# A joint ring for the q and k projections, 1 KB weight rows in two slots, and a smaller preference for attention in the list scheduler

## The chip, the core and the metric

The kernel runs on one core of a Trainium2 chip. The metric is the device time of one execution in microseconds. The core has five engines with a queue of instructions each: TensorE (PE, matmuls), VectorE (DVE), ScalarE (ACT), GpSimd (POOL) and SyncE (SP). Every engine works through its queue in order; between engines there are semaphores. DMAs are issued from the queues of SP and POOL and carried out by 16 DMA engines that both share.

## The reference, cut to what matters

```python
x = A_x                                  # 1 x 2048 x 576, bf16
xn = _layernorm(x)
s = _A_ref(xn, A_wqkv, A_wo)             # attention: 32 heads of 18, each query sees the 256 keys up to itself
g = _silu(_B_ref(xn, w_gate, w_up, w_down))
return x + s * g

# _A_ref
qkv = (x @ wqkv).reshape(B, S, 3, H, Dh)         # D = 576, so q, k and v have 576 columns each
scores = einsum(q, k) * Dh ** -0.5, masked to 0 <= i - j < 256
o = softmax(scores) @ v
return o @ wo
# _B_ref, F = 4608
h = sigmoid(x @ w_gate) * (x @ w_up)
return h @ w_down
```

## The kernel before, in words

**Tiling.** The 2048 tokens are cut into four chunks of `NT` = 512. For each chunk the builder makes the operations of one pipeline: layer norm and transposes into `xnT` (`build_ln`), the v projection (`build_v`), the q/k projection (`build_qk`, five column groups `gi` of 128), attention for eight head groups `hg` of four heads (`build_attn`), the output projection (`build_wo`) and the FFN (`build_ffn`). All contractions over 576 are done as nine pairs of matmuls with 64 rows each; the two of a pair run side by side in the upper and lower half of the array (`pair`, line 88, which is why nearly all of TensorE's work has that line).

**q and k.** `build_qk` projects 128 columns of q and of k at once into one PSUM unit, and a VectorE copy (line 517) puts them into `qd[:, slot, 0 or 1, :]`, a ring of two slots. Heads are 18 columns wide and the attention wants each at a multiple of 32 partitions, so every head is spread by DMA: one from the q half into `qT` (a ring of four slots, one per head group in flight), one from the k half into `kT`. All of these are issued from POOL's queue through the helper `dma` (line 232). `kT` holds, for every head group, three units of 256 keys; two hold the current chunk and one the second half of the chunk before, and `unit_slot` and `sub_pos` say which. The projection of group `gi` needs the slot of `qd` that the spreads of `gi - 2` have to have read. `build_attn` then makes `kx`, two copies of all 768 keys with every second head set to zero (line 595, two VectorE instructions per head group, ring of two), computes five batches of scores, exponentials on ScalarE (line 626), masks on VectorE, and the product with v (`pv`).

**FFN.** F = 4608 is 36 tiles of 128 (`ft`). `weights(wg)` loads the columns of `WG` = 2 tiles of gate (to partitions 0 to 63) and of up (to 64 to 127) into one of `NWS` = 4 slots of `wgs` with two DMAs from SP's queue; a row of such a load is 2 x 128 x 2 bytes = 512 B. A slot is released when its last tile has been multiplied. `gate_up` is one half of a tile's gate/up work, `tail` the tanh and the product that give `hT`. `down` is the second projection, `build_final` the gate, the residual and the store. In chunk 0 the first three tiles are worked in two halves of the tokens before the attention can begin. All weights are read again in every chunk, except `wd_sb`, which stays.

**Order.** Nothing is ordered by hand. `schedule` is a list scheduler that runs at build time with estimated durations: at each step it takes, for the engine that can start earliest, the operation with the least `start + prio * PRIO_NS`; attention has priority 1, gate/up and down steps 3. It estimates 600 ns for a DMA's issue, lands it 2.5 us later, and not before the bytes of all earlier DMAs have passed at 205 bytes per ns. The order it finds is then fixed for every engine: a step whose operand is later than planned stops everything behind it on its engine.

```python
DMA_ISSUE_NS = {"SP": 600.0, "POOL": 600.0, "ACT": 650.0}
DMA_LAT_NS = 2500.0
DMA_BYTES_PER_NS = 205.0
...
k = (st + o.prio * self.PRIO_NS, o.cidx)
```

The functions that the diff touches, and what calls them:

Of the kernel before, what the change touches and what calls it, by code (L numbers as in the profile page):

```python
# [20 lines left out]
BPC = NT // P  # L21
FG = 4
NFG = NFT // FG
WG = 2
NWS = 4
EPS = 1e-5
SM_SCALE = float(DH) ** -0.5

# [2 lines left out]
NVS = 12  # L31
VH = DH + 1
VSZ = (H // 2) * VH
NOT = 1
NQS = 4
NKX = 2
NEX = 8
# [25 lines left out]
def mm_ns(n):  # L63
    return max(24.7, n / 2.4 + 2.7)
# [136 lines left out]


class Builder:
    PRIO_NS = 80.0

    def __init__(self, nc, x_ap, wqkv_ap, wo_ap, wg_ap, wu_ap, wd_ap, out_ap, verbose=False):
        self.nc = nc
# [28 lines left out]
    def alloc_memory(self):  # L236
        nc = self.nc
        bf16, f32 = dt.bfloat16, dt.float32
        cur = [(nc.sbuf_base + 63) // 64 * 64]
        top = nc.sbuf_top  # L240

        def size(shape, dtp):
            n = 1
            for s_ in shape[1:]:
                n *= s_
            return n * mybir.dt.size(dtp)

        def seq(name, shape, dtp=bf16, align=32):
            off = (cur[0] + align - 1) // align * align
            cur[0] = off + size(shape, dtp)  # L250
            assert cur[0] <= top, f"out of SBUF at {name}: {cur[0]} > {top}"
            return nc.alloc_sbuf_tensor_at(name, list(shape), dtp, offset=off), off

        self.xnT, _ = seq("xnT", [P, 2, KS, NT])
        self.wd_sb, _ = seq("wd_sb", [P, NFT, D])
        self.hT, _ = seq("hT", [P, NFT, NT])
        self.wgs, _ = seq("wgs", [P, NWS, 9, WG * P])
        self.tring, _ = seq("tring", [P, 2, NT])
        self.v_aug, _ = seq("v_aug", [P, NVS * VSZ + VH])
        self.qT, _ = seq("qT", [P, NQS, NT])  # L260
        self.kT, _ = seq("kT", [P, NHG, 12 * SW])
        self.kx, _ = seq("kx", [P, NKX, 12, 2, SW])
        self.expr, zex = seq("expr", [P, NEX, 2, NT])
        self.x0 = nc.alloc_sbuf_tensor_at("x0", [P, BPC, D], bf16, offset=zex)
        assert size([P, BPC, D], bf16) <= size([P, NEX, 2, NT], bf16)
        self.o_tok, _ = seq("o_tok", [P, BPC, XW])
        self.oT, _ = seq("oT", [P, NOT, KS, P])
        self.s_attn, _ = seq("s_attn", [P, BPC, D])
        self.wqk, _ = seq("wqk", [P, KS, XW])
        self.wv_sb, _ = seq("wv_sb", [P, KS, D // 2])  # L270
        self.wo_sb, _ = seq("wo_sb", [P, KS, D // 2])
        self.qd, _ = seq("qd", [P, NQD, 2, NT])
        self.xr, _ = seq("xr", [P, NXR, D])
        self.xnr, _ = seq("xnr", [P, NXN, XW])
        self.xf, _ = seq("xf", [P, NFIN, D])
        self.thf, _ = seq("thf", [P, NFIN, D])
        self.ident, _ = seq("ident", [P, SW])
        self.mask, _ = seq("mask", [P, P])
        self.small, _ = seq("small", [P, 3 + 16 * NST], f32)
        sm = self.small  # L280
        self.neghalf, self.half = sm[:, 0:1], sm[:, 1:3]
        self.bnst = sm[:, 3:3 + 12 * NST].rearrange("p (s i c) -> p s i c", i=2, c=6)
        self.mv = sm[:, 3 + 12 * NST:3 + 14 * NST].rearrange("p (s c) -> p s c", c=2)
        self.veps = sm[:, 3 + 14 * NST:3 + 15 * NST].rearrange("p (s c) -> p s c", c=1)
        self.rstd = sm[:, 3 + 15 * NST:3 + 16 * NST].rearrange("p (s c) -> p s c", c=1)
        self.pvs, _ = seq("pvs", [P, 1, 4 * BPC * (DH + 1)], f32)
        if self.verbose:
            print(f"SBUF used up to {cur[0]} of {top} ({top - cur[0]} free)")
        self.ps = nc.alloc_psum_tensor("ps", [P, 4096], f32)
        self.psb = self.ps.bitcast(bf16)  # L290
        self.pool_s = Pool("S", [0, 1])
        self.pool_f = Pool("F", [2, 3])

    def build_graph(self):
# [14 lines left out]
        self.op_xnT = [[] for _ in range(NC)]  # L309
        self.op_v = {}  # L310
        self.op_vis = {}
        self.op_kx = {}
        self.last_vis = None
        self.ffn_last = None
        self.op_pv = {}
# [85 lines left out]
    def build_attn_consts(self):  # L401
# [3 lines left out]
        o = op("POOL", 400, lambda e: e.memset(vv[:, :, DH:VH], 1.0), "init:vones", deps=d, prio=1)  # L405
        self.op_vones = o
        self.op_vzero = o = op("POOL", 100, lambda e: e.memset(self.v_aug[:, NVS * VSZ:NVS * VSZ + VH], 0.0), "init:vzero", deps=[o], prio=1)
        self.op_qz = o = op("POOL", 1600, lambda e: e.memset(self.qT[:, :, :], 0.0), "init:qz", deps=[o], prio=1)
        self.op_kz = o = op("POOL", 6200, lambda e: e.memset(self.kT[:, :, :], 0.0), "init:kz", deps=[o], prio=1)
        lo = slice(0, SW)  # L410
        o = op("POOL", 150, lambda e: e.memset(self.mask[lo, :], 1.0), "init:m0", deps=[o], prio=1)
        o = op("POOL", 200, lambda e: e.affine_select(self.mask[lo, 0:SW], self.mask[lo, 0:SW], pattern=[[-1, SW]],
# [83 lines left out]
    def build_qk(self, c, gi):  # L496
# [24 lines left out]
        for u in range(H):  # L521
            lo, hi = max(DH * u, gi * P), min(DH * u + DH, (gi + 1) * P)
            if lo >= hi:
                continue
            hg, p0 = u // 4, 32 * (u % 4) + lo - DH * u
            for w in range(2):
                if w == 0:
                    if (c, hg) not in self.q_slot:
                        self.q_slot[(c, hg)] = self.r_q.produce()
                    qs, war = self.q_slot[(c, hg)]  # L530
                    war = [war, self.op_qz]
                    dst = self.qT[p0:p0 + hi - lo, qs, :]
                else:
                    war = [self.op_kx[(c - 1, hg)]] if c else [self.op_kz]
                    n1 = unit_slot(c, 1)
                    dst = self.kT[p0:p0 + hi - lo, hg, :].rearrange("p (u t) -> p u t", u=3)[:, 0:n1 + 1:n1, :]
                s0, sb = (lo - gi * P, w) if gi < 4 else (lo - gi * P + 64 * w, 0)
                src = self.qd[s0:s0 + hi - lo, sq, sb, :]
                if w:
                    src = src.rearrange("p (u t) -> p u t", u=2)  # L540
                o = self.dma(dst, src, (hi - lo) * NT * 2, f"dma:sp:{c}:{u}:{w}:{gi}", ("qk", par, gi),
                             deps=[ev, war], prio=1, eng="POOL")
                self.op_sp.setdefault((c, hg), []).append(o)
                self.sp_grp.setdefault((c, gi), []).append(o)
                self.r_qd.release(sq, o)
                self.hg_grps.setdefault((c, hg), set()).add(gi)

    def row_proj(self, eng, h, lhs, w):
        res = None
# [34 lines left out]
    def build_attn(self, c, hg):  # L584
# [4 lines left out]

        sx, dx = self.r_kx.produce()  # L590
        kxo = []
        for t in range(2):
            def f_kx(e, t=t):
                src = self.kT[:, hg, :].rearrange("p (s k) -> p s k", k=SW)
                return e.tensor_scalar(self.kx[:, sx, :, t, :], src, self.half[:, t:t + 1], None, ALU.mult)  # L595
            kxo.append(op("DVE", dve_ns(12 * SW, 4.0), f_kx, f"kx:{c}:{hg}:{t}", deps=[sp, dx, self.op_kz, self.op_half], prio=1))
        self.op_kx[(c, hg)] = kxo

        where = {}
        ready = []  # L600
# [1 line left out]
        for vi, (specs, groups) in enumerate(zip(bins, masks)):  # L602
# [3 lines left out]
            def f_sc(eng, specs=specs, h=h):  # L606
                res = None
                outs = self.halves(h, NT)
                for ks, q0, nq in specs:
                    kp = sub_pos(c, ks)  # L610
                    cols = slice(q0 * SW, (q0 + nq) * SW)
                    res = pair(eng, [b[:, cols] for b in outs],
                               lambda r, t: self.kx[r, sx, kp, :, :].rearrange("p t k -> p (t k)"),
                               lambda r, t: self.qT[r, qs, cols], True, True)
                return res
            sc = op("PE", sum(mm_ns(nq * SW) for _, _, nq in specs), f_sc, f"sc:{c}:{hg}:{vi}",
                    deps=[sp, kxo, self.r_ex.rel[self.r_ex.uses % NEX]], prio=1, acq=h, odeps=[self.last_vis])
# [36 lines left out]
        def f_pv(eng):  # L654
# [22 lines left out]
                    res = pair(eng, [b[:, o + VH:o + 3 * VH].rearrange("p (k d) -> p k d", k=2) for b in outs],  # L677
                               lambda r, i: self.expr[r, se, t, qb * P:(qb + 1) * P], two, True, True)
            return res
        pv = op("PE", 40 * 24.7, f_pv, f"pv:{c}:{hg}", deps=[[m for m, _ in ready], vdeps, self.op_vzero], prio=1, acq=hp)  # L680
        self.op_pv[(c, hg)] = pv
        for se in sorted({se for _, se in ready}):
            self.r_ex.release(se, pv)
# [67 lines left out]
    def build_ffn(self, c):  # L751
# [13 lines left out]

        def weights(wg):
            sw, dw = self.r_w.produce()
            pr = 1 + wg if c == 0 and wg < 4 else 3
            fc = slice(wg * WG * P, (wg + 1) * WG * P)
            ds = self.load_rows(self.wgs[:, sw, :, :], self.wg[:, fc], self.wu[:, fc], f"dma:w:{c}:{wg}", ("w", sw), pr, [dw])  # L770
            slots[wg] = sw
            wops[wg] = ds

        def load_wd(fg):
            self.op_wd.append(self.dma(
# [8 lines left out]
        def gate_up(ft, h, half, acq, part=None):  # L784
# [6 lines left out]
            def f(eng):  # L791
                res = None
                outs = [bank(h, w)[:, t0:t0 + n] for w in range(2)]
                for k in ks:
                    res = pair(eng, outs, lambda r, t: self.wgs[r, sw, SUB[t][k], fc], lambda r, t: x_in[r, k, t0:t0 + n],
                               k == 0, k == KS - 1)
                return res
            return pe(len(ks) * mm_ns(n), f, f"f1{half}:{c}:{ft}", [xin, wops[ft // WG]], acq,
                      3 if part is None else 1)

        def tail(ft, h, pg):
# [12 lines left out]
        if early:  # L814
            weights(0)
            weights(1)
            hs = [self.pool_f.hold() for _ in range(2)] + [self.pool_s.hold()]
            for part in range(2):
                for ft in range(early):
                    gate_up(ft, hs[ft], 0, None if part else hs[ft], part)  # L820
                    u = gate_up(ft, hs[ft], 1, None, part)
                    if part:
                        tail(ft, hs[ft], u)
                    if part and ft == 1:
                        self.r_w.release(slots[0], u)
        for ft in range(early, NFT):
            if ft % WG == 0 and ft // WG not in slots:
                weights(ft // WG)
# [266 lines left out]
```

## Time and profile before

| | |
|---|---|
| time, median of three | 591.35 us (590.41 to 591.4) |
| span of the profiled execution | 591.4 us |
| TensorE's granted clock, mean | 0.995 |
| gate/up matmuls (`ps<-xnT,wgs`) | 2646, 302.6 us of records |
| down matmuls (`ps<-wd_sb,hT`) | 2304, 153.4 us |
| spreading DMAs issued by POOL | 144 to `qT` (75.8 us), 144 to `kT` (80.7 us) |
| `kx` multiplies on VectorE, 768 columns | 64, 24.5 us |
| weight loads `wgs` | 144 of 288 KB |

A span of a matmul in the trace holds its whole way through the array, so that neighbours overlap; what a stretch of matmuls costs is read from the starts. A pair of 64 x 512 matmuls follows the one before it after 216 ns. In the page, L88 is any matmul, L232 any DMA issue; the names of the tiles tell them apart. `SPq` and `POOL` with DMA_DIRECT2D are issues, not transfers.

### The profile page before, as it was taken

The page shows a single profiled execution, that of the slowest core. Times are in us where ns is not written, and L with a number is a line of the kernel's source. Part 1 is how long each engine was busy: PE and PEld are TensorE (multiplying, and loading weights), DVE is VectorE, ACT ScalarE, POOL GpSimd, SP SyncE. Part 2 cuts the span into 40 slices and gives each one's busy share as a digit, 9 for nine tenths or more (in the row PEclk, how much of TensorE's full clock was granted, in tenths as well). Part 3 has the DMA queues.
Part 4 walks back from the last instruction along what each step waited for, and adds up shares of the span by engine and source line. Part 5 has one row for each costly group of instructions (what it writes and reads, how often), then busy time and mean ns, then how long its engine had stood idle before and what let it go on. Part 6 is the DMA issues. An engine that isn't in the chain of part 4 may idle for free.

```text
span 591.4 us, 21879 instructions
## 1 busy us (share of the span) xinstructions
PE 575.2 (97%) x9774; PEld 366.3 (62%) x9774; DVE 347.7 (59%) x832; ACT 279.8 (47%) x389; POOL 173.7 (29%) x318
## 2 busy tenths in 40 slices
PE   8889999999999999999999999999999999999996
PEld 7545555687785556456677765555557864444775
DVE  5447869964679878477776347887631233333122
ACT  3234857642378774267775247668420022332111
POOL 5495630007980300984200296450000000000000
PEclk9999999999999999999999999999999999999999
DMA  9999998731214553456301025465461116763010
GB/s 200 193 214 195 202 184 198 175 87 40 71 28 102 118 147 82 105 125 139 91 4 43 8 53 131 121 138 121 112 156 32 32 44 154 166 161 81 2 43 21
DMA packets 112046, 63.82 MB, mean 108 GB/s; under 512 B 12208, under 2 KB 109936, under 8 KB 111952
## 3 DMA queue, kind: packets, MB, share of 16 engines
q1 hardware_dynamic: 102736, 57.67, 43.2%
q0 software_dynamic: 9216, 4.75, 4.0%
q8 instruction: 77, 1.26, 1.0%
q14 instruction: 17, 0.14, 0.1%
HBM read 55.30 MB, written 2.36 MB: 97 GB/s over the span
## 4 chain that ended last, share of the span: by engine, by line
PE 89%; DMA 4%; POOL 3%; SPq 2%; DVE 1%; issue 1%; ACT 0%; DVEq 0%
PE ps L88 88%; DMA kT<-qd 2%; DMA wqk<-in_A_wqkv_dram 2%; SPq L232 2%; POOL qT L232 1%; POOL kT L232 1%; PE ps L480 1%; DVE qd L517 0%; DVE s_attn L890 0%; DVE thf L895 0%; DVE hT L806 0%; ACT tring L803 0%; DVE xf L900 0%; DVE xnr L451 0%; DVEq L1023 0%
## 5 line engine op out<-in xcount | busy, mean ns | idle before, releaser
L88 PE MATMUL ps<-xnT,wgs 64*128 64x512 bf16 (+1 forms) x2646 | 302.6, 372 | 2.7 <-DVE xnr L451 1.4
L88 PEld LDWEIGHTS ps<-xnT,wgs 64*128 64x128 bf16 x2646 | 128.8, 94 | 123.5 <-DVE xnr L451 1.5
L626 ACT ACTIVATE expr<-ps 128x1024 bf16<-128x1024 f32 (+2 forms) x160 | 152.4, 985 | 51.2 <-PE ps L88 50.9
L88 PE MATMUL ps<-wd_sb,hT 64*128 64x288 bf16 x2304 | 153.4, 283 | 1.3 <-issue 1.3
L806 DVE SCALAR_TENSOR_TENSOR hT<-tring,ps 128x512 bf16<-128x512 bf16 x144 | 98.8, 686 | 84.4 <-ACT tring L803 81.4
L803 ACT ACTIVATE tring<-ps 128x512 bf16<-128x512 f32 x144 | 86.2, 599 | 114.5 <-PE ps L88 111.9
L88 PEld LDWEIGHTS ps<-wd_sb,hT 64*128 64x128 bf16 x2304 | 111.4, 94 | 28.3 <-issue 1.6
L232 POOL DMA_DIRECT2D qT<-qd x144 | 75.8, 528 | 118.1 <-PE ps L88 74.9
L232 POOL DMA_DIRECT2D kT<-qd x144 | 80.7, 562 | 11.8 <-DVE qd L517 11.4
L639 DVE TENSOR_TENSOR expr<-expr,mask 128x256 bf16<-128x256 bf16 (+2 forms) x232 | 62.5, 292 | 30.3 <-ACT expr L626 29.1
L692 DVE TENSOR_REDUCE pvs<-ps 64x304 f32<-64x608 f32 x64 | 50.4, 788 | 10.7 <-PE ps L88 9.5
L88 PE MATMUL ps<-qT,kx 64*128 64x320 bf16 (+4 forms) x736 | 56.7, 252 | 0.0
L880 ACT ACTIVATE thf<-ps 128x576 bf16<-128x576 f32 (+1 forms) x20 | 11.1, 555 | 76.2 <-PE ps L88 75.9
L88 PEld LDWEIGHTS ps<-qT,kx 64*128 64x128 bf16 x736 | 30.8, 94 | 24.7 <-issue 2.5
L88 PE MATMUL ps<-xnT,wqk 64*128 64x512 bf16 (+1 forms) x360 | 39.4, 363 | 5.7 <-DMA kT<-qd 2.7
L88 PEld LDWEIGHTS ps<-v_aug,expr 64*128 64x128 bf16 x2432 | 35.2, 93 | 6.4 <-issue 0.8
L443 POOL TENSOR_TENSOR small<-small 128x1 f32<-128x1 f32 x16 | 9.2, 580 | 94.0 <-DVE small L441 93.9
L88 PE MATMUL ps<-v_aug,expr 64*128 64x19 bf16 (+1 forms) x2432 | 36.0, 170 | 0.2 <-issue 0.2
L88 PEld LDWEIGHTS ps<-xnT,wqk 64*128 64x128 bf16 x360 | 18.1, 95 | 23.7 <-issue 8.1
L883 DVE SCALAR_TENSOR_TENSOR thf<-thf,ps 128x576 bf16<-128x576 bf16 x12 | 9.0, 749 | 38.2 <-ACT thf L880 38.1
L517 DVE CAST qd<-ps 128x1024 bf16<-128x1024 f32 (+1 forms) x20 | 22.3, 1116 | 13.2 <-PE ps L88 13.1
L595 DVE TENSOR_SCALAR kx<-kT,small 128x768 bf16<-128x768 bf16 x64 | 24.5, 408 | 5.8 <-DMA kT<-qd 5.2
(52 smaller groups left out, 262.2 us busy)
## 6 DMA issues: line engine op xcount, KB each, us to landing
wgs<-in_B_w_gate_dram SPq DMA_DIRECT2D x72, 288.0 KB, 4.0
wgs<-in_B_w_up_dram SPq DMA_DIRECT2D x72, 288.0 KB, 4.9
wd_sb<-in_B_w_down_dram SPq DMA_DIRECT2D x9, 576.0 KB, 8.9
xf<-in_A_x_dram SPq DMA_DIRECT2D x16, 144.0 KB, 2.2
out_dram<-xf SPq DMA_DIRECT2D x16, 144.0 KB, 1.8
qT<-qd POOLq DMA_DIRECT2D x112, 18.0 KB, 2.6
kT<-qd POOLq DMA_DIRECT2D x112, 18.0 KB, 2.5
xr<-in_A_x_dram SPq DMA_DIRECT2D x6, 288.0 KB, 3.9
```

The source lines that it names most:

```text
L88: res = eng.matmul(outs[i], lhs(ROWS[t], i), rhs(ROWS[t], i), start=start, stop=stop, tile_position=(64 * t, 0))
L232: o = self.op(eng, DMA_ISSUE_NS[eng], lambda e: e.dma_start(dst, src), name, deps, prio, nbytes=nbytes)
L443: rs = op("POOL", 560, lambda e, ss=ss: e.tensor_tensor(self.rstd[:, ss, :], self.veps[:, ss, :], self.neghalf[:, :], ALU.pow), f"ln:rs:{s ...
L517: return eng.tensor_copy(dst, self.both(h, n))
L595: return e.tensor_scalar(self.kx[:, sx, :, t, :], src, self.half[:, t:t + 1], None, ALU.mult)
L626: return eng.activation(self.expr[:, se, :, lo * SW:NT], self.both(h, NT)[:, :, lo * SW:NT], ACTF.Exp, scale=SM_SCALE)
L639: return eng.tensor_tensor(e_, e_, m_, ALU.mult)
L692: return eng.tensor_reduce(out[ROWS[i]], src, mybir.AxisListType.X, ALU.add)
L803: th = op("ACT", act_ns(NT), lambda e: e.activation(self.tring[:, st, :], bank(h, 0), ACTF.Tanh, scale=0.5), f"th:{c}:{ft}", deps=[pg, dt_ ...
L806: mu = op("DVE", dve_ns(NT), lambda e: e.scalar_tensor_tensor(self.hT[:, ft, :], self.tring[:, st, :], 1.0, bank(h, 1), ALU.add, ALU.mult) ...
L880: return e.activation(v2(t)[:, a:b, :], y2()[:, a:b, :], ACTF.Tanh, scale=0.25)
L883: q1 = op("DVE", dve_ns(D), lambda e: e.scalar_tensor_tensor(v2(t), v2(t), 1.0, y2(), ALU.add, ALU.mult), f"fq1:{sb}", deps=[th, f2], prio=0)
```

## The change

It has five parts, and the first pays with its SBUF for some of the others.

- **A joint ring.** `qT` and the current chunk's part of `kT` become one tile `qk[:, slot, 0 or 1, :]`, laid out as `qd` is, so that one DMA spreads the q and the k of a head (2 KB per partition). Only column group 4, where q and k lie on different partitions, still takes two. The second half of the chunk before is kept in `kprev`, copied there on POOL once its `kx` has been made; the part of `kx` that comes from it is made on POOL, the rest on VectorE. A slot of the ring is released by the scores and by that copy.
- **1 KB weight rows.** `WG` = 4 and `NWS` = 2: the same SBUF in two slots of four tiles, loads of twice the size and half the number. In chunk 0 the first slot is filled by two loads of two tiles with a semaphore each, so that the first tiles need not wait for all of it.
- **A smaller preference.** `PRIO_NS` goes from 80 to 10, so that two steps of priority are worth 20 ns of start time in place of 160.
- **Two buffers for `oT`**, the transposed attention output.
- **An order for `pv`.** In chunks after the first, the product with v of head groups 1 to 7 comes after the last transpose of the chunk before.

```diff
-WG = 2
-NWS = 4
+WG = 4
+NWS = 2
...
-NOT = 1
+NOT = 2
...
-    PRIO_NS = 80.0
+    PRIO_NS = 10.0
...
-        self.qT, _ = seq("qT", [P, NQS, NT])
-        self.kT, _ = seq("kT", [P, NHG, 12 * SW])
+        self.qk, _ = seq("qk", [P, NQS, 2, NT])
+        self.kprev, _ = seq("kprev", [P, NHG, NT // 2])
...
-        self.op_qz = o = op("POOL", 1600, lambda e: e.memset(self.qT[:, :, :], 0.0), "init:qz", deps=[o], prio=1)
-        self.op_kz = o = op("POOL", 6200, lambda e: e.memset(self.kT[:, :, :], 0.0), "init:kz", deps=[o], prio=1)
+        self.op_qz = o = op("POOL", 4300, lambda e: e.memset(self.qk[:, :, :, :], 0.0), "init:qz", deps=[o], prio=1)
+        self.op_kz = o = op("POOL", 2200, lambda e: e.memset(self.kprev[:, :, :], 0.0), "init:kz", deps=[o], prio=1)
...
+            if gi < 4:
+                moves = [(self.qk[p0:p0 + n_, qs, :, :], self.qd[s0:s0 + n_, sq, :, :])]
+            else:
+                moves = [(self.qk[p0:p0 + n_, qs, w, :], self.qd[s0 + 64 * w:s0 + 64 * w + n_, sq, 0, :]) for w in range(2)]
...
+        for eng, src, pos, n_ in (("DVE", self.qk[:, qs, 1, :], 4, NT), ("POOL", self.kprev[:, hg, :], 0, NT // 2)):
+            for t in range(2):
+                def f_kx(e, t=t, src=src, pos=pos, n_=n_):
+                    return e.tensor_scalar(self.kx[:, sx, pos:pos + n_ // SW, t, :], src.rearrange("p (s k) -> p s k", k=SW),
+                                           self.half[:, t:t + 1], None, ALU.mult)
+                kxo.append(op(eng, dve_ns(n_, 4.0) if eng == "DVE" else 400, f_kx, f"kx:{c}:{hg}:{t}",
+                              deps=[sp if eng == "DVE" else self.op_kp.get(hg), dx, self.op_kz, self.op_half], prio=1))
+        self.op_kp[hg] = op("POOL", 300, lambda e: e.tensor_copy(self.kprev[:, hg, :], self.qk[:, qs, 1, NT // 2:NT]),
+                            f"kp:{c}:{hg}", deps=[kxo, sp], prio=2)
+        self.r_q.release(qs, self.op_kp[hg])
...
-        pv = op("PE", 40 * 24.7, f_pv, f"pv:{c}:{hg}", deps=[[m for m, _ in ready], vdeps, self.op_vzero], prio=1, acq=hp)
+        pv = op("PE", 40 * 24.7, f_pv, f"pv:{c}:{hg}", deps=[[m for m, _ in ready], vdeps, self.op_vzero, self.otr_last if hg else None], prio=1, acq=hp)
...
-            pr = 1 + wg if c == 0 and wg < 4 else 3
+            pr = 1 + 2 * wg if c == 0 and wg < 2 else 3
+            parts = 2 if c == 0 and wg == 0 else 1
```

More of the change, by code (lines that the diff above doesn't have):

```diff
@@ L311, in build_graph @@
         self.op_vis = {}
-        self.op_kx = {}
+        self.op_kp = {}
         self.last_vis = None
@@ L524, in build_qk @@
                 continue
[L525 to L542, printed above, removed]
+            hg, p0, n_ = u // 4, 32 * (u % 4) + lo - DH * u, hi - lo
+            if (c, hg) not in self.q_slot:
+                self.q_slot[(c, hg)] = self.r_q.produce()
+            qs, war = self.q_slot[(c, hg)]
+            s0 = lo - gi * P
+            if gi < 4:
+                moves = [(self.qk[p0:p0 + n_, qs, :, :], self.qd[s0:s0 + n_, sq, :, :])]
+            else:
+                moves = [(self.qk[p0:p0 + n_, qs, w, :], self.qd[s0 + 64 * w:s0 + 64 * w + n_, sq, 0, :]) for w in range(2)]
+            for w, (dst, src) in enumerate(moves):
+                o = self.dma(dst, src, n_ * 2 * NT * 2 // len(moves), f"dma:sp:{c}:{u}:{w}:{gi}", ("qk", par, gi),
+                             deps=[ev, war, self.op_qz], prio=1, eng="POOL")
                 self.op_sp.setdefault((c, hg), []).append(o)
@@ L545, in build_qk @@
                 self.r_qd.release(sq, o)
-                self.hg_grps.setdefault((c, hg), set()).add(gi)
+            self.hg_grps.setdefault((c, hg), set()).add(gi)
     def row_proj(self, eng, h, lhs, w):
@@ L591, in build_attn @@
         kxo = []
[L592 to L597, printed above, removed]
+        for eng, src, pos, n_ in (("DVE", self.qk[:, qs, 1, :], 4, NT), ("POOL", self.kprev[:, hg, :], 0, NT // 2)):
[8 more added lines that the diff above has]
+        self.r_q.release(qs, self.op_kp[hg])
         where = {}
@@ L609, in f_sc @@
                 for ks, q0, nq in specs:
-                    kp = sub_pos(c, ks)
+                    kp = ks + 4
                     cols = slice(q0 * SW, (q0 + nq) * SW)
@@ L613, in f_sc @@
                                lambda r, t: self.kx[r, sx, kp, :, :].rearrange("p t k -> p (t k)"),
-                               lambda r, t: self.qT[r, qs, cols], True, True)
+                               lambda r, t: self.qk[r, qs, 0, cols], True, True)
                 return res
@@ L767, in weights @@
             sw, dw = self.r_w.produce()
-            pr = 1 + wg if c == 0 and wg < 4 else 3
-            fc = slice(wg * WG * P, (wg + 1) * WG * P)
-            ds = self.load_rows(self.wgs[:, sw, :, :], self.wg[:, fc], self.wu[:, fc], f"dma:w:{c}:{wg}", ("w", sw), pr, [dw])
+            pr = 1 + 2 * wg if c == 0 and wg < 2 else 3
+            parts = 2 if c == 0 and wg == 0 else 1
+            w = WG // parts
+            for i in range(parts):
+                fc = slice((wg * WG + i * w) * P, (wg * WG + i * w + w) * P)
+                ds = self.load_rows(self.wgs[:, sw, :, i * w * P:(i + 1) * w * P], self.wg[:, fc], self.wu[:, fc],
+                                    f"dma:w:{c}:{wg}:{i}", ("w", sw, i), pr + i, [dw])
+                for ft in range(wg * WG + i * w, wg * WG + i * w + w):
+                    wops[ft] = ds
             slots[wg] = sw
-            wops[wg] = ds
         def load_wd(fg):
@@ L797, in f @@
                 return res
-            return pe(len(ks) * mm_ns(n), f, f"f1{half}:{c}:{ft}", [xin, wops[ft // WG]], acq,
+            return pe(len(ks) * mm_ns(n), f, f"f1{half}:{c}:{ft}", [xin, wops[ft]], acq,
                       3 if part is None else 1)
@@ L823, in build_ffn @@
                         tail(ft, hs[ft], u)
-                    if part and ft == 1:
-                        self.r_w.release(slots[0], u)
         for ft in range(early, NFT):
```

## The prediction, made before the change was run

> **What bounds the kernel now.** I read the page's busy shares first, then who waits for whom on TensorE, before and after 150 us, then the stage with the largest wait, and last the weight loads, because the change halves the number of their buffers.
>
> ```profile
> PE 575.2 (97%) x9774; PEld 366.3 (62%) x9774; DVE 347.7 (59%) x832; ACT 279.8 (47%) x389; POOL 173.7 (29%) x318
> ...
> DMA  9999998731214553456301025465461116763010
> ```
>
> TensorE (PE) has something running 97% of the time, no other engine passes 62%, and the DMA engines are full only in the first sixth. The waits of TensorE, first 0 to 150 us, then 150 to 590:
>
> ```profile
> PE ps L88 <- DMA kT<-qd: 2.4, 1, 2.4
> PE ps L88 <- DMA wqk<-in_A_wqkv_dram: 1.9, 1, 1.9
> PE ps L88 <- issue: 1.8, 2, 1.1
> PE ps L88 <- DVE xnr L451: 1.4, 1, 1.4
> PE ps L88 <- DVE hT L382: 1.1, 1, 1.1
> PE ps L88 <- ACT xnT L466: 0.6, 1, 0.6
> ```
>
> ```profile
> PE ps L88 <- issue: 1.5, 2, 1.3
> PE ps L88 <- DMA kT<-qd: 0.2, 1, 0.2
> ```
>
> All waits together are 10.9 us of 591, and 9.2 of them lie before 150 us. So nothing the change does to ACT, DVE or POOL can pay by itself: a gain must come out of those 9 us, and a loss can come anywhere, because the order on TensorE is fixed at build time and one late operand stops everything behind it. The largest wait, in the timeline of TensorE and in a table of stretches (PE, PEld, DVE, ACT and POOL busy, then granted clock, DMA share, GB/s):
>
> ```profile
> 35.66 4.50 PE L88 MATMUL ps<-xnT,wgs 64*128 64x512 bf16 x40
> 42.60 3.45 PE L88 MATMUL ps<-xnT,wqk 64*128 64x512 bf16 x18 [2.44 <-DMA kT<-qd]
> ```
>
> ```profile
> 36.00:40.00 4.00, 4.00 (x40) 1.92 (x34) 1.37 (x2) 1.19 (x2) 4.00 (x9) 1.00 1.17 207
> 40.00:43.20 3.20, 0.76 (x8) 0.37 (x8) 0.71 (x3) 0.60 (x1) 3.01 (x6) 1.00 1.18 180
> 43.20:46.70 3.50, 3.50 (x25) 1.70 (x22) 1.25 (x3) 0.18 (x1) 0.00 (x0) 0.51 1.14 194
> ```
>
> The third q/k projection of chunk 0 needs the projection buffer `qd` that the spreading DMAs of the first still read. It waits 2.44 us, and then TensorE gets half the clock for 3.4 us, which costs about 1.7 more: 4.1 us for one late DMA. The chain of waits shows why it is late: POOL issues 16 DMAs one after the other, 26.74 to 34.43, and the last takes 8 us to land:
>
> ```profile
> 26.74 0.72 POOL qT L232
> ...
> 34.43 8.04 DMA kT<-qd
> ```
>
> Now the weights, in a stretch of pure gate/up work, 484 to 540 us (median to landing from each issue), and the same in chunk 0, 45 to 80 us:
>
> ```profile
> wgs<-in_B_w_gate_dram SPq DMA_DIRECT2D x14, 288.0 KB, 4.0
> wgs<-in_B_w_up_dram SPq DMA_DIRECT2D x14, 288.0 KB, 4.5
> ```
>
> ```profile
> DMA packets 11261, 7.06 MB, mean 202 GB/s; under 512 B 1172, under 2 KB 10981, under 8 KB 11255
> ...
> wgs<-in_B_w_up_dram SPq DMA_DIRECT2D x6, 288.0 KB, 10.9
> ...
> wgs<-in_B_w_gate_dram SPq DMA_DIRECT2D x5, 288.0 KB, 10.6
> ```
>
> The reader is to see two regimes: 4 to 5 us to land when the queue is free, 11 us when it is full. Today a pair of F tiles is fetched six tiles ahead, and no gate/up matmul waits for it.
>
> **What the Trainium skill says.** (1) "DMA: Bandwidth & Descriptors", Why small descriptors are slow: a descriptor of n bytes costs n/32 beats plus about 3. That makes 2 x 19 = 38 beats for 1 KB in 512 B rows and 35 in one row: an estimate of 8% less. The trace agrees in kind: alone, a 512 B packet takes 34 ns and a 1152 B one about 65, which is 15% less per byte. Where the queue is full (10 to 20 us) 512 B took 44 and 1 KB 88: nothing gained. (2) "TensorE: Matmul & The Clock Gate", What's actually happening: the clock is full or half, decided per window of some 3.4 us by how busy the array was; the 0.51 above agrees. (3) "GPSIMD Engine Reference", Elementwise: 1.8 cycles an element at 1.2 GHz at best. (4) "SBUF — State Buffer", Who interferes with whom: VectorE in a two-port mode or with two SBUF inputs blocks GpSimd for a whole instruction. No row of this trace shows a GpSimd copy, so (3) and (4) are untested here.
>
> **The change, part by part.**
>
> *Joint q/k ring.* Per chunk 72 spreading DMAs become 32 joint ones and 8 single ones: 288 become 160. At 0.53 to 0.56 us of POOL each (75.8 / 144 and 80.7 / 144) that removes 128 x 0.545 = 70 us. Added on POOL are two halving multiplies and one copy per head group, 96 of 256 columns. By (3) each is 256 x 1.8 / 1.2 = 384 ns plus start; the smallest real POOL operation here, an affine_select of 64 columns, took 239 ns. I take 0.55 us, from 0.3 to 1.0 with blocking as in (4): 53 us (29 to 96). POOL ends near 155 us, far from a bound either way. It works in order, though: a multiply that waits for a free `kx` buffer holds back the spreads behind it, as spreads that wait for a `qT` buffer do today. On VectorE, 64 multiplies of 768 columns (408 ns) become 512: 256 / 4 / 0.96 = 67 ns less each, 4 us, beside TensorE. The start-up memsets (5.2 + 1.8 us, done by 17.3 us) shrink to about 5.4, beside the loads.
>
> What counts is the start. Eight issues go out in 0.72 + 7 x 0.5 = 4.2 us, the last at 30.5. The old DMA issued at 30.46 landed at 37.3, so I put the last joint one at 37.4 (35 to 39: twice the bytes each, but fewer weights queued ahead): 5 us sooner than 42.5. The planner will also ask for it sooner. It books 600 ns per issue, 4.8 us less, but lands no DMA before the bytes queued ahead of it at 205 GB/s; with the queue full that clock, not the issues, sets its date, so I expect it to move the projection by about 3 us, to a place where the data is there. I take the wait and the slow clock as gone: -4.1 us (from 0 to -4.1).
>
> *Two slots of four F tiles.* Same bytes, same SBUF. The load is now requested four tiles ahead instead of six and is twice as large. Pure stretch: one F tile is 9 pairs of matmuls at 216 ns, 1.944 us, four are 7.78. A matmul's record (376 ns) runs 0.16 us into its successor, so from release to need there are 7.6 us. The load: the pair of DMAs is complete 0.64 + 4.5 = 5.1 us after the first issue, and 288 KB of that is 0.64 + 4.5 - 4.0, about 1.2 us of transfer, so the fixed part is 5.1 - 2.4 = 2.7. Twice the bytes makes 2.7 + 4.8 = 7.5 us at the old packet rate, 7.1 with the 8% of (1), 6.8 with the 15% of the trace. I take 7.1: it fits with 0.5 to spare. Of the 14 pairs in this stretch about four took 0.4 to 1.0 longer than 5.1, so of seven loads here and two at 420 to 440 some two come late by about 0.3: +0.6 us. At 7.5 all nine would graze the limit: +2.5.
>
> Chunk 0: the queue is full, so bytes count. Tiles 18 and 19 were issued at 50.9, landed at 63.8 and were used at 67.8. Now tiles 16 to 19 come as one slot, issued when tile 11 is done (50.9), and are wanted at tile 16, which started at 62.4. The same bytes queued give 63.8: +1.4 us. After that four tiles take 10.2 to 12.4 us with the attention between them, and 1.18 MB at 202 GB/s plus 2.7 is 8.5, up to 10.5 with a `wd_sb` load ahead: I count no more (up to 1 us in each of six groups).
>
> *The rest costs nothing.* PRIO_NS lowers the preference of attention (priority 1 against 3) from 160 to 20 ns. It can save only waits for attention, and after 150 us there are none; it can delay an attention step by half a gate/up tile, about 1.1 us, and the last spread is issued at 398 us with 190 us of FFN to come. The second `oT` buffer and the order of `pv` after the last transpose touch work that TensorE fills with FFN steps.
>
> Sum: -4.1 + 1.4 + 0.6 = -2.1, so 589.2 us.
>
> **The rivals.** *The weight ring becomes the bound.* For: half the depth, in-order TensorE, 0.5 us to spare on an estimate. Against: the 10 us spacing in mixed stages. Half the start gain (-2), 4 us in chunk 0 and 2.5 in pure stretches: 595.9. *The gain is handed to the next wait.* For: chunk 0 moves 202 GB/s and cannot deliver sooner, so what starts sooner waits longer at tile 16. Against: attention is ready to fill in. The start gain of 4.1 is spent there: 591.3. *All the start shrinks.* 1 KB rows bring `wqk` sooner and the new order steps over the 1.4 us wait for `xnr`: -4.1 - 1.9 - 1.4 + 0.6 = -6.8, 584.6. Against: the queue at 10 to 20 us gave 1 KB rows nothing.
>
> **How the numbers follow.** Forecast 0.40 and large gain 0.13 are faster: 0.53. Handed on is 0.14: the same. Ring bound is 0.33: slower. The range runs from 584 (large gain) to 598 (ring bound with two more late groups), leaving about 0.06 outside at each end.
>
> **What would show it.** Right: the 2.4 us wait for `kT<-qd` and the clock of 0.51 near 43 us are gone, 160 spreads, weight pairs that land in about 7.1 us at the end, a new wait of TensorE for `wgs` of some 2 us in all. Wrong: `wgs` waits above 5 us, or a wait for POOL's `kx`, or the `qd` wait of the old size at an earlier time.

## The result and the profile after

The changed kernel took 595.41 us (593.98 to 596.95) against 591.38 (590.41 to 591.68): ratio 1.0072, interval 1.0043 to 1.01. It is slower by 4.0 us where 2.1 us less were forecast. The profiled executions do not lie at the medians: that of the kernel before took 593.09 us, 1.7 above its median, that of the changed one 593.98, 1.4 below, so the two traces differ by 0.9 us and not by 4.0.

The page and the waits of TensorE of the changed kernel, first 0 to 150 us, then from 150 on:

```profile
PE 575.6 (97%) x9788; PEld 395.1 (67%) x9788; DVE 348.3 (59%) x832; ACT 280.4 (47%) x389; POOL 176.3 (30%) x286
...
q8 instruction: 77, 1.26, 0.9%
```

```profile
PE ps L88 <- issue: 1.8, 2, 1.4
PE ps L88 <- DVE hT L382: 1.1, 1, 1.1
PE ps L88 <- ACT xnT L466: 0.5, 1, 0.5
PE ps L88 <- DMA wgs<-in_B_w_up_dram: 0.4, 1, 0.4
PE ps L88 <- DMA wqk<-in_A_wqkv_dram: 0.3, 1, 0.3
```

```profile
PE ps L88 <- issue: 3.3, 4, 1.5
PE ps L88 <- DMA qk<-qd: 1.6, 1, 1.6
PE ps L88 <- DVE pvs L690: 1.2, 1, 1.2
PE ps L88 <- DVE expr L637: 0.9, 1, 0.9
```

The reader is to see that the waits have moved. The 2.4 us for a spread, 1.9 for `wqk` and 1.4 for `xnr` are gone or small, and the half clock is gone, as the same stretches show (granted clock third from the end):

```profile
40.00:43.20 3.20, 3.20 (x40) 1.78 (x38) 2.50 (x6) 2.60 (x4) 1.42 (x3) 1.00 1.10 219
43.20:46.70 3.50, 3.50 (x58) 1.74 (x56) 2.80 (x10) 3.50 (x6) 1.86 (x4) 1.00 1.10 262
```

In their place stand 7.0 us of waits after 150 us, where the kernel before had 1.7. The weight loads from 484 to 545 us, and TensorE beside SP's queue around one slot:

```profile
wgs<-in_B_w_gate_dram SPq DMA_DIRECT2D x7, 576.0 KB, 5.3
wgs<-in_B_w_up_dram SPq DMA_DIRECT2D x7, 576.0 KB, 7.4
```

```profile
493.72 9.10 PE L88 MATMUL ps<-xnT,wgs 64*128 64x512 bf16 x80
503.61 8.59 PE L88 MATMUL ps<-xnT,wgs 64*128 64x512 bf16 x78 [0.78 <-issue]
```

```profile
494.79 0.59 SPq L232 DMA_DIRECT2D wgs<-in_B_w_gate_dram  x1
495.43 0.64 SPq L232 DMA_DIRECT2D wgs<-in_B_w_up_dram  x1
498.43 0.82 SPq L232 DMA_DIRECT2D xf<-in_A_x_dram  x2
```

At the medians a slot is full 0.64 + 7.4 = 8.0 us after its first issue, not 7.1. The slot issued at 494.79, the slowest of this stretch, with two loads for `xf` issued behind it, landed at 503.51, and TensorE went on at 503.61. The view puts that wait down to "issue", since it did not find the landing; that the wait ended 0.1 us after a slot had landed, at the first matmul of the slot's first tile, is what tells it. Seven tiles wait in this way after 400 us.

For a count by cause I took every gap between the starts of two matmuls that was more than 0.1 us over their normal spacing, from 12 us on. *Weights*: it ended at the first matmul of a tile, within 0.45 us of a slot's landing. *No semaphore*: the matmul waits for nothing; the part in brackets is only the wider spacing of matmuls while the clock is at half. *Other*: it waits for something else. In us, good to some 0.5, since they depend on what is taken as normal:

| profile of | weights | no semaphore | other, before 150 us | other, 150 to 400 us |
|---|---|---|---|---|
| kernel before | 0 | 4.4 (1.0) | 6.4 | 0.9 |
| changed kernel | 3.5 | 4.1 (0) | 0.8 | 4.5 |
| changed kernel, again | 5.3 | 8.3 (1.2) | 0.6 | 4.8 |
| frozen order, two waits a slot | 0 | 3.6 (1.2) | 3.1 | 3.3 |
| frozen order, one wait a slot | 4.7 | 2.9 (1.0) | 2.1 | 2.9 |
| two waits a slot, freely planned | 0 | 2.8 (1.3) | 2.9 | 1.5 |
| old ring of four slots, else changed | 0 | 3.4 (1.3) | 3.1 | 4.0 |
| the same with PRIO_NS = 80 | 0 | 6.9 (0.9) | 1.0 | 5.0 |

The sum of the normal spacings is the same in both kernels to within 0.2 us: the work of TensorE didn't change, only its gaps.

### The profile page after: what moved, and what is told of

Its sections match the earlier page's. It is cut to its first block, busy times and chain, and to the rows that moved or that the text cites. A ratio compares the mean times of both kernels' runs of the same rounds, so it can differ in the third digit from the quotient of the medians.

```text
span 592.2 us, 21831 instructions
## 1 busy us (share of the span) xinstructions
PE 575.6 (97%) x9788; PEld 395.1 (67%) x9788; DVE 348.3 (59%) x832; ACT 280.4 (47%) x389; POOL 176.3 (30%) x286
## 3 DMA queue, kind: packets, MB, share of 16 engines
q8 instruction: 77, 1.26, 0.9%
## 4 chain that ended last, share of the span: by engine, by line
PE 88%; DMA 5%; issue 2%; POOL 2%; SPq 1%; DVE 1%; POOLq 0%; DVEq 0%
PE ps L88 86%; DMA qk<-qd 3%; DMA wqk<-in_A_wqkv_dram 2%; SPq L232 1%; POOL qk L232 1%; PE ps L480 1%; POOL kx L589 1%; DVE pvs L690 0%; DVE qd L517 0%; DVE s_attn L891 0%; DVE thf L896 0%; DVE xf L901 0%; POOL kprev L593 0%; DVE expr L637 0%; POOLq L1024 0%
## 5 line engine op out<-in xcount | busy, mean ns | idle before, releaser
L88 PEld LDWEIGHTS ps<-xnT,wgs 64*128 64x128 bf16 x2646 | 139.4, 94 | 116.0 <-issue 9.5
L88 PEld LDWEIGHTS ps<-wd_sb,hT 64*128 64x128 bf16 x2304 | 124.4, 94 | 15.3 <-issue 1.7
L232 POOL DMA_DIRECT2D qk<-qd x160 | 82.3, 523 | 96.1 <-DVE qd L517 61.7
L589 POOL TENSOR_SCALAR kx<-kprev,small 128x256 bf16<-128x256 bf16 x64 | 64.0, 1009 | 61.6 <-PE ps L88 61.0
L637 DVE TENSOR_TENSOR expr<-expr,mask 128x256 bf16<-128x256 bf16 (+2 forms) x232 | 65.1, 304 | 27.4 <-ACT expr L624 26.1
L88 PE MATMUL ps<-qk,kx 64*128 64x320 bf16 (+4 forms) x736 | 59.3, 251 | 1.2 <-DVE pvs L690 1.2
L88 PEld LDWEIGHTS ps<-qk,kx 64*128 64x128 bf16 x736 | 32.5, 94 | 23.3 <-DVE pvs L690 1.7
L589 DVE TENSOR_SCALAR kx<-qk,small 128x512 bf16<-128x512 bf16 x64 | 22.8, 383 | 11.2 <-DMA qk<-qd 9.5
L571 ACT ACTIVATE v_aug<-ps 64x288 bf16<-64x288 f32 x32 | 13.1, 408 | 23.2 <-PE ps L88 22.8
```

What stands on the lines that cost most here:

```text
L88: res = eng.matmul(outs[i], lhs(ROWS[t], i), rhs(ROWS[t], i), start=start, stop=stop, tile_position=(64 * t, 0))
L232: o = self.op(eng, DMA_ISSUE_NS[eng], lambda e: e.dma_start(dst, src), name, deps, prio, nbytes=nbytes)
L571: return eng.activation(dst, src, ACTF.Copy)
L589: return e.tensor_scalar(self.kx[:, sx, pos:pos + n_ // SW, t, :], src.rearrange("p (s k) -> p s k", k=SW), self.half[:, t:t + 1], None, A ...
L637: return eng.tensor_tensor(e_, e_, m_, ALU.mult)
```

## The experiments

Three theories. R: the two-slot weight ring costs the loss. P: the multiplies on POOL cost it. O: the order that the planner finds costs it. Where no base is named the edit is to the changed kernel; ratios are to the kernel before, run beside it on the same chip, with 95% intervals. The changed kernel had 1.0072 at first and 1.014 on another chip (below), so differences of up to 0.7% between runs on different chips show little; those on one chip decide.

**The old ring** (`e_w2`).

```diff
-WG = 4
-NWS = 2
+WG = 2
+NWS = 4
```

(with the old `weights` and its release of slot 0.)

> The changed kernel with the old weight ring (WG = 2, NWS = 4, 512 B rows), all else as changed. Theory R (the two-slot ring costs the loss): the waits of TensorE inside gate/up work at 420 to 553 us, 3.1 us in the profile of the changed kernel, go, and the median falls by 3 us or more, to 592.5 or below. Theory P (the multiplies of kx on POOL cost it): no more than 1 us better, 594.5 or above, with the waits near 230, 246 and 376 us still there. Theory O (the order that PRIO_NS = 10 makes costs it): as P.

Measured 0.9985 (0.9962 to 1.0007), median 592.08. The waits for weights are gone, and with them 0.9% against the first run of the changed kernel: as R expects.

**Two waits for a slot** (`e_halves`, and on another chip `e_halves_again`).

```diff
-            parts = 2 if c == 0 and wg == 0 else 1
+            parts = 2
```

> The changed kernel with two slots of four tiles, but every slot filled by two loads of two tiles (512 B rows) with a semaphore each, so that the first two tiles wait only for the first half. Theory R by lateness: the second half is wanted 3.9 us later, so the waits at 420 to 553 us go as in the run with the old ring, about 3 us better, 592.5 or below. Theory R by prefetch depth alone (release four tiles ahead): no better than 1 us. Theories P and O: 594.5 or above.

Measured 0.9911 (0.9879 to 0.9942), median 588.16: the release four tiles ahead stays, and all of the loss goes and more, as R by lateness expects and R by depth does not. It also beats the kernel before. The planner's order changes with this edit, and the rows are short again; both are held apart below.

**The multiplies on VectorE** (`e_kxdve`).

```diff
-        for eng, src, pos, n_ in (("DVE", self.qk[:, qs, 1, :], 4, NT), ("POOL", self.kprev[:, hg, :], 0, NT // 2)):
+        for eng, src, pos, n_ in (("DVE", self.qk[:, qs, 1, :], 4, NT), ("DVE", self.kprev[:, hg, :], 0, NT // 2)):
...
-                              deps=[sp if eng == "DVE" else self.op_kp.get(hg), dx, self.op_kz, self.op_half], prio=1))
+                              deps=[sp if pos else self.op_kp.get(hg), dx, self.op_kz, self.op_half], prio=1))
```

> The changed kernel with the two multiplies for the kept keys on VectorE in place of POOL. Theory P: POOL's 64 us of multiplies are gone, spreads are issued on time, and the waits near 230, 246 and 376 us (1.8 + 1.4 + 1.1 = 4.3 us in the profile of the changed kernel) go: 591.5 or below. Theory R: no better than 1 us, 594.5 or above, with the waits at 420 to 553 us unchanged.

Measured 1.0085 (1.006 to 1.011), median 597.07, where P expected 591.5 or below. Counted as in the table, 4.3 us of other waits between 150 and 400 us remain, against 4.5: taking POOL's largest new group, below, away did not remove them. Since the changed kernel did not run on this chip, the ratio alone would not settle P; the same edit where no tile waits for weights, further down, does.

```profile
L232 POOL DMA_DIRECT2D qk<-qd x160 | 82.3, 523 | 96.1 <-DVE qd L517 61.7 <-PE ps L88 32.9 <-issue 1.0
L589 POOL TENSOR_SCALAR kx<-kprev,small 128x256 bf16<-128x256 bf16 x64 | 64.0, 1009 | 61.6 <-PE ps L88 61.0
```

**The old preference** (`e_prio80`: `PRIO_NS = 80.0`).

> The changed kernel with PRIO_NS = 80. Theory O: attention is asked for earlier again and at least 2 us come back, 593.4 or below. Theories R and P: within 1 us of the changed kernel, 594.4 to 596.4, with both groups of waits still there, at other places in the attention stages since the order is another.

Measured 1.0167 (1.0125 to 1.021), median 602.0, slower than all three theories expected. The smaller preference helps the changed kernel: by 0.9% against its first run, by 0.3% against its second.

**The ring on the kernel before** (`e_before_w4`, the weights of the changed kernel in the kernel before), and **the preference on the kernel before** (`e_before_prio10`: `PRIO_NS = 10.0`).

> The kernel before with the new weight ring alone (WG = 4, NWS = 2, first slot in two loads). Theory R: gate/up tiles wait for their load in every pure stretch, 3 us at 420 to 553 us, and some in chunk 0: ratio to the kernel before 1.005 to 1.012. If the loss belongs to the joint ring or the new order instead: ratio 0.998 to 1.002.

> The kernel before with PRIO_NS = 10 alone. The prediction gave this no effect, since TensorE waits for no attention step after 150 us: ratio 0.998 to 1.002. Theory O (the order counts by itself): the run with PRIO_NS = 80 on the changed kernel was 0.8% slower than the changed one, so the ratio here would be 0.99 to 0.995.

Measured 1.0138 (1.0078 to 1.0199) and 0.9967 (0.9944 to 0.999). The ring alone costs at least as much as the whole change; the preference alone gains 0.3%, which is small, but its interval leaves out 1.

**The preference and the multiplies where no tile waits** (`e_halves_prio80`, `e_halves_kxdve`: two waits a slot, with one more edit each).

> The changed kernel with slots filled in two loads and PRIO_NS = 80. Theory O: about 0.8% above the run with two loads and PRIO_NS = 10, which had the ratio 0.991 to before, so about 0.999. If the larger preference only hurt by asking for gate/up tiles at a time when the two-slot ring had not delivered: within 0.3% of 0.991.

> The changed kernel with slots filled in two loads and the multiplies for the kept keys on VectorE. Theory P on a base without ring waits: POOL loses 64 multiplies of 1.0 us, spreads are issued sooner, 1 to 2 us better than the run with two loads alone, ratio 0.988 or below. If POOL's multiplies are hidden: 0.990 to 0.993. If VectorE's order behind a late operand is worse than POOL's: above 0.994.

Measured 0.9947 (0.9926 to 0.9967) and 0.9914 (0.9882 to 0.9946). The preference is worth 0.4% here, with intervals that still touch; whether the late ring adds to its worth on the changed kernel is not shown. POOL's 64 us of multiplies are hidden: against 0.9911, and 0.9919 on another chip, moving them gains nothing, and theory P falls.

**The same order with two waits** (`e_frozen`, `e_frozen_again`). The instruction order of TensorE, VectorE, ScalarE and POOL is written out from the changed kernel's plan:

```diff
+                if e in ORDER:
+                    want = ORDER[e][len(prog[e])] if len(prog[e]) < len(ORDER[e]) else None
+                    cand = [o for o in cand if o.name == want]
...
-            parts = 2 if c == 0 and wg == 0 else 1
+            parts = 2
```

> The order of every instruction on TensorE, VectorE, ScalarE and POOL is exactly that of the changed kernel; only each weight slot is filled by two loads of two tiles with a semaphore each. What is gained here over the changed kernel is the lateness of the weights alone; what the freely planned run with two loads gained beyond it (ratio 0.991 to before, against 1.007) is the order. Theory R by lateness: the waits inside gate/up work (5.4 us in the profile of the changed kernel) go and nearly all is gained, ratio 0.991 to 0.995. If most of it was the order: 1.000 to 1.005.

**The changed kernel beside it** (`e_after_again`).

> The changed kernel itself again, beside the others on one chip. All theories: ratio 1.004 to 1.010 as measured before.

Measured on one chip: 0.9981 (0.9957 to 1.0005) frozen, between the two ranges expected, and 1.014 (1.0101 to 1.018) as changed, above the range expected. With not one compute instruction moved, shorter rows and a second wait take back 1.6%, 9.8 us of the medians. Of that the two traces show 5.3 us of weight waits and 4.7 us of gaps without a semaphore. Why the changed kernel was slower here than at first (1.0072) is open.

**Short rows, one wait** (`e_frozen_all4`): the frozen order and 512 B rows, but all four tiles wait for both loads.

```diff
-                for ft in range(wg * WG + i * w, wg * WG + i * w + w):
-                    wops[ft] = ds
+                for ft in range(wg * WG, wg * WG + WG):
...
+                        wops.setdefault(ft, []).extend(ds)
```

> The order of the changed kernel again, slots filled by two loads of two tiles in 512 B rows, but all four tiles of a slot wait for both loads (the first slot of chunk 0 apart). If the one wait for four tiles is what costs: the waits inside gate/up work are back, above 3 us at 420 to 553 us, and the ratio to before is 1.005 to 1.014, as for the changed kernel. If the 1 KB row is what costs: as the run with the frozen order and two waits, 0.996 to 1.001.

> The frozen order with two loads and two waits per slot again, beside the other two. Ratio 0.996 to 1.001 as before, if the chip makes no difference.

> The changed kernel with two loads and two waits per slot, freely planned, again, beside the frozen order on one chip. If the order adds to the gain: 0.990 to 0.994 as before, against 0.998 with the frozen order. If the difference was the chip's: 0.996 to 0.999.

Measured on one chip: 1.0071 (1.0047 to 1.0094) with one wait, 0.9973 (0.9951 to 0.9994) with two, 0.9919 (0.9896 to 0.9942) with two and free planning. Here the view finds the landings of the five longest waits and names them, TensorE from 400 to 556 us:

```profile
PE ps L88 <- DMA wgs<-in_B_w_up_dram: 2.5, 5, 0.8
```

So it is the one wait for four tiles, with short rows as with long: 1.0%, or 4.9 us of the medians, of which the table's weight waits are 4.7. The frozen kernel with one wait has two loads a slot and 512 B rows, so neither the row nor the number of loads is needed for the loss. The remaining 0.5% between frozen and free is the order.

**Two waits on the kernel before** (`e_before_halves`), and **the joint ring with the `oT` buffers and the order of `pv`** (`e_w2_prio80`: old ring and old preference).

> The kernel before with two slots of four tiles, each filled by two loads of two tiles, all else as before. The ring alone with one load per slot had ratio 1.014. Theory R by lateness: with two loads the ring is no worse than the four slots of two, 0.997 to 1.003. If releasing four tiles at once is a cost of its own: 1.004 or above.

> The joint ring, two oT buffers and the order of pv, with the old weight ring and PRIO_NS = 80. If the joint ring brings the 4 us at the start that the prediction gave it: 0.993 to 0.996. If its POOL multiplies and its later waits give that back: 0.998 to 1.003.

Measured 0.9997 (0.9969 to 1.0024): two slots with two waits are as good as four slots, to within 0.3%. And 1.0006 (0.9976 to 1.0036): the joint ring without the new weight ring and preference brings nothing. The table shows where its start gain went in the profiled execution (595.61 us, 2.0 above its median): other waits before 150 us fall from 6.4 to 1.0, but waits without a semaphore rise from 4.4 to 6.9 and the later ones from 0.9 to 5.0. Two of its gaps, in the timeline of TensorE:

```profile
72.38 1.46 PE L88 MATMUL ps<-xnT,wgs 64*128 64x512 bf16 x11
75.62 1.03 PE L88 MATMUL ps<-xnT,wgs 64*128 64x512 bf16 x7 [1.79 <-issue]
...
80.91 1.31 PE L88 MATMUL ps<-xnT,wgs 64*128 64x512 bf16 x10
85.25 1.89 PE L88 MATMUL ps<-xnT,wgs 64*128 64x512 bf16 x8 [3.03 <-issue]
```

Both lie inside a tile, where a matmul waits for nothing. In each a 16 KB packet of the queue "instruction" is in flight (72.7 to 74.0 and 82.4 to 83.8 us), and each ends 1.5 or 1.6 us after that packet. It is so every time: from 12 us on the 17 profiles of this case have 68 gaps of more than 0.15 us before a matmul that waits for no semaphore (half clock left out), and all 68 ended 1.2 to 1.7 us after the end of such a packet, a stretch that makes up some 8% of the time. Waits with a semaphore ended anywhere from 0 to 19 us after one. All 77 such packets together are 1.26 MB, 64 B for each of the 19,548 matmuls and weight loads recorded of the kernel before, so I read them as TensorE's own program arriving late. That reading is argued from times and sizes; no run took these fetches away.

## Why the prediction was wrong

**The step that failed: "I take 7.1: it fits with 0.5 to spare", and from it "+0.6 us".** The window of 7.6 us rests on a spacing that held: where no tile waits, slots are issued 7.8 us apart (491.89, 499.67 and 507.44 in `e_halves`). The load was mis-sized: 8.0 us. Its fixed part was right, its transfer was not. The two halves of a slot land 0.64 + 7.4 - 5.3 = 2.7 us apart, so 1.18 MB take some 5.5 us, where the old packet rate gave 4.8, and 2.5 are left. I had taken 8% off for the 1 KB row, an estimate from the Trainium skill, "DMA: Bandwidth & Descriptors", Why small descriptors are slow. The measurement says otherwise. SP's queue (packets, MB, share of 16 engines) in the pure stretch, kernel before (56 us) and changed (61 us):

```profile
q1 hardware_dynamic: 16862, 8.55, 64.2%
```

```profile
q1 hardware_dynamic: 8576, 8.55, 66.0%
```

That is 34 ns a packet before and 75 after, a few small packets included; those of 1 KB alone took 77 ns on average, two of 512 B 68, so nothing comes off. My own lines for the full queue, 44 and 88 ns, had said the same. Even my upper end was low: with short rows and two pairs queued the same 1.18 MB took 7.8 us (488.38 to 496.20 in the run with one wait), a 512 B packet taking 39 ns. With the window missed by a few tenths seven slots are late, not two of nine: 3.3 us after 400 us in the first trace and 5.3 in the second, for the 0.6 predicted. By the medians the one wait costs more, 4.9 us with short rows and, beside the changed kernel, 9.8.

This was my rival "the weight ring becomes the bound". That its 595.9 lies next to the measured 595.41 is luck: it was the sum of -2 at the start, +4 in chunk 0 and +2.5 in pure stretches, and the traces show neither of the first two.

**Chunk 0, +1.4: not seen.** The slot of tiles 16 to 19 landed at 61.18 and was used at 61.32, just in time; from 12 us on weight waits before 150 us are 0.2 us. The load itself took 12.4 us from its first issue, near the 12.9 that I had (50.9 to 63.8). But it was issued at 48.8, not at 50.9, since TensorE was through with tile 11 at 48.4: my step kept the old date of the release after the start had been moved forward. With the same ring on the kernel before (`e_before_w4`), TensorE did wait 2.0 us for weights before 150 us:

```profile
PE ps L88 <- DMA wgs<-in_B_w_up_dram: 2.0, 3, 1.6
```

With two waits the two-slot ring is quicker here than the old one. Median landings from 45 to 80 us, joint ring with PRIO_NS = 80, first the old ring, then two slots with two waits:

```profile
wgs<-in_B_w_gate_dram SPq DMA_DIRECT2D x6, 288.0 KB, 11.2
wgs<-in_B_w_up_dram SPq DMA_DIRECT2D x5, 288.0 KB, 12.1
```

```profile
wgs<-in_B_w_gate_dram SPq DMA_DIRECT2D x6, 288.0 KB, 8.1
wgs<-in_B_w_up_dram SPq DMA_DIRECT2D x6, 288.0 KB, 8.5
```

**The start, -4.1: right, but not kept.** The wait and the half clock are gone, and the last of the first eight joint spreads landed at 37.1 (predicted 37.4). Of the other waits there `xnr` went too. That for `wqk` only looks gone, as the two chains show, before and changed:

```profile
12.12 10.80 DMA wqk<-in_A_wqkv_dram
22.92 0.14 issue
23.05 2.13 PE ps L88 x18
```

```profile
9.70 13.45 DMA wqk<-in_A_wqkv_dram
23.15 0.14 issue
23.28 38.00 PE ps L88 x582
```

The weights landed no sooner, and the projection began 0.2 us later. Its wait is short because TensorE had stood still before it, 1.4 us of that without a semaphore, up to 19.2. And what was gained was lost again: the joint ring on the old weight ring and preference came out at 1.0006.

**The late waits, costed at nothing: wrong.** From 150 to 400 us 3.6 us were added. The traced ones before 232 and 248 us end with spreads that took 4.7 to 7.4 us to land, where two of the first group that were issued ahead of the weight load took 1.8 and 1.9; the 1.18 MB slots were issued at 221.8 and 237.6. But a slot's load beside the spreads is not enough for it: two waits a slot, freely planned, ask for the same bytes at once and have 1.5 us of such waits, while the changed order keeps 3.3 with two waits, and the old ring, else changed, has 4.0. So most of it goes with the order, and why that order has them is open. They are not POOL's multiplies, though these were mis-sized: 1009 ns each for my 0.55 us (upper end 1.0), far above the 384 ns plus start of the prediction's (3), and moving them gained nothing. Whether VectorE blocked them, as in (4), no run shows.

**PRIO_NS, costed at nothing: wrong by 0.3% on the kernel before,** and by 0.4%, less surely, with two waits a slot.

The sum by measured terms: -5.6 for other waits before 150 us, +3.5 for weights, +3.6 in the middle, -0.3 without a semaphore (half clock -1.0, gaps +0.7) gives +1.2 us, near the difference of the two traces (0.9 us), not of the medians (4.0 us). In the second trace of the changed kernel weights are 1.8 us and gaps without a semaphore 4.2 us larger; the rest of the 4.0 has no trace of its own. By the medians the account is shorter: the changed kernel with two waits a slot and its order frozen is 1.1 and 1.6 us faster than the kernel before, the first not clear of noise, and the one wait costs 9.8 and 4.9.

## What to carry to other kernels

A buffer's size, its release and the wait for it are three things: two slots of four tiles were as good as four of two once each half had its own semaphore. Before making a load larger, compare its time with the stretch between release and use, with the durations of this trace at the number of loads that will be queued; a margin of 0.5 us in 7.1, on an estimate, was in truth 0.4 us missing. A wait that shrinks in the trace is a gain only if the work behind it also begins sooner. Here the gain at the start was lost again where what came next, spreads and perhaps the program itself, was no earlier; the best version, two waits a slot with the rest as changed, is 0.8 to 0.9% faster than the kernel before.

## What the runs showed of the hardware

- A 1 KB packet of these weight loads took 77 ns on average in the changed kernel and 79 in its second trace, two of 512 B 68 with one pair of loads queued and 78 with two: no gain from the longer row.
- A deeper queue was not faster. From 40 to 60 us the four-slot ring moved 196 GB/s and the two-slot ring with two waits 231 (joint ring, PRIO_NS = 80); 214 and 232 with PRIO_NS = 10; 191 and 225 on the kernel before. From 24 to 100 us all of them moved 199 to 206. The DMA engines finished one 288 KB load up to 5 us apart in the first of these (47.93 to 53.12), 3 to 4 us apart in the second.
- TensorE stood still before matmuls that wait for nothing, 1.2 to 7.5 us in all per execution with the half clock left out, and every such gap over 0.15 us ended 1.2 to 1.7 us after a 16 KB instruction packet.
- A POOL multiply of 256 columns by a column of factors took 1009 ns, a POOL copy of the same size 431.
